# The second expert block of a fused attention and two-expert kernel: output transposed in 384-token columns, Strassen factors formed on the way in, and one list schedule for both blocks

## The chip, the cores and the metric

One core of one Trainium2 chip runs the whole program. The metric is device time in microseconds of one launch. The engines are PE (matmul, with its weight loads shown apart as PEld), DVE, ACT and POOL (elementwise work) and SP, which only issues DMAs. Each engine runs its own instructions strictly in program order and waits on the others by semaphores, so where an instruction is put on its engine decides what waits behind it.

## What is computed

```python
def _attn_ref(q, k, v):          # chunks of 64, softmax(q k / 8) v
def _moe_ref(x, w_in, w_out, g_ln):
    h = x @ w_in                 # 4608 x 512 by 512 x 1024
    solu = h * softmax(h)
    ln = (solu - mean) / sqrt(var + 1e-06) * g_ln
    return ln @ w_out            # 1024 x 512
def _moe2_ref(x, w_in, w_out):
    h = x @ w_in                 # 4608 x 512 by 512 x 2048
    g = h * (1.0 / (1.0 + np.exp(-h)))
    return g @ w_out             # 2048 x 512
```

`reference` runs the three one after the other on 4608 tokens. The four weight matrices arrive as 64-bit numbers and are turned into fp32 on the chip, in 48 pieces of 128 x 512 (512 KB each).

## The kernel before

The program has three stretches on PE. **Stage one** is attention plus the first expert block, in 36 tiles of 128 tokens: `attend`, `weigh` (softmax), `moe_in` (L499, 24 matmuls of 512 columns a tile), `norm` (L506 maximum, L510 exp, L512 product), `turn_ln` (L533 transposes) and, for every 4 tiles, four `moe_out` (L544, 24 matmuls of 512 columns each). **Way in** is the second block's first matrix product: 6 groups of 768 tokens, 8 units a group, a unit being 256 of the 2048 features. **Way out** is its second product, for 18 pairs of token tiles (256 tokens).

Every big product is done in fp32r with operands split into a high and a low part, three passes (`PASSES`: high by high, high by low, low by high); a split is one ACT copy (high) and one subtraction on DVE or POOL (low). Both products of the second block use the seven-product Strassen form (`SEVEN` = p1, p6, p2, p7, p5, p4, p3): sums of the quarter blocks of each operand are formed first, seven products are made, and their sums give the four quarters of the result.

- Weights. `convert` takes a 64-bit piece through five DVE instructions (L292, L295, L309, L314, L345) and one ACT instruction (L297). For the pieces of stage one, letters in `SUM_ON` and `LOW_ON` say whether the sum (L314) and the low part (L363) go to DVE, to POOL or through PE (E). `w2_mix` then forms the seven weight factors of two pieces on POOL (L395, four sums of 128 x 256) and splits them (L408 on ACT or L406 on POOL, and L410 on POOL), and stores both parts to HBM (`w2d`, `w2od`). The 16 pieces of the way in's matrix are done in stage one, the 16 of the way out's during the way in.
- Way in. `raw_load`, `raw_t` (L594, POOL) and `s_split` (L619 ACT, L623 DVE or POOL) make the seven operands of a group. `product` (L656) is 6 matmuls of 384 columns; a unit pair is 14 products in turn. The results are summed as they come: `c_p1` (L669), `c_u2` (L673), `c_u3` (L677), `c22` (L687), `c21` (L695), `c12` (L703), with silu on ACT. PE may write p7 only after `c_u2` has read the bank, and p3 only after `c22` has. Each unit stores four quarters of 192 KB to `gd` (L664), on SP.
- Way out. `g_load` brings the silu output back (four DMAs of 512 KB a pair), `g_sum` (L758, two on DVE and two on POOL, 128 x 1024) forms the sums, `g_split` (L769 ACT, L771 DVE or POOL) splits seven operands, and `out_product` (L778) makes 24 matmuls of 256 columns with the token block as the stationary operand:

```python
for f in range(NF):
    for i, (a, c) in enumerate(PASSES):
        nc.tensor.matmul(acc, g[:, a, f, :], wo2[o, f][:, c, :], ...
```

- Order. For stage one a planner (`Steps`, filled by `stage_one`) holds every operation with its engine, its assumed length, its needs and its due time, and `solve` list-schedules them; the start times order each engine's instructions. `NOMINAL`, `WAY_OUT` and `W2_FROM` set due times only. The way in and the way out are placed by hand, by offsets from the end of stage one (`XA`, `XB`, `FIRST_LOADS`, `FIRST_SUMS`, `FIRST_SPLITS`).

Of the kernel before, what the change touches and what calls it, by code (L numbers as in the profile page):

```python
# [43 lines left out]
class Steps:  # L44


    LATENCY = {"PE": 0.2, "DVE": 0.06, "ACT": 0.06, "POOL": 0.08, "DMA": 1.9, "SP": 0.0}
# [16 lines left out]
    def solve(self):  # L64
# [20 lines left out]
        engines = {st["engine"] for st in self.steps}  # L85
# [5 lines left out]
        while events:  # L91
# [42 lines left out]
def stage_one(T, way_out, w2_from, tiles=36, per=4, ahead=2):  # L134

    step = Steps(dict(S=1, X=1, tr=2, y=2, h=1, u=4, xs=2, e=2, pT=2, qk=3, v=2, ln=2, ys=2, st=2, cv=2, cvs=2))
    op = step.op
    dma = lambda kb, **more: ("DMA", kb * 1024 / 300e3, more)
# [5 lines left out]
    for i in range(32):  # L144
# [11 lines left out]
        due = T[w2_from] + (T[tiles - 2] - T[w2_from]) * (i - 16) / 16  # L156
        steps[-1][2].update(give=[("w", i)], due=due)
        op("convert", (i,), *steps)
        if i % 2:
            steps = [("POOL", 0.74, dict(need=[("w", i - 1), ("w", i)] if n == 0 else [])) for n in range(4)]  # L160
            for n in (512, 512, 256, 512):
                steps += [("ACT", 0.17 + n / 1200, dict(take=["cvs"])), ("POOL", 0.2 + n * 0.0021, {}), sp(n // 256 if n > 256 else 1), dma(n, free=["cvs"])]
            steps[-1][2].update(free=["cvs", "cv", "cv"], due=due + 22)
            op("w2_mix", ((i - 17) // 2, 0), *steps)
    for t in range(-ahead, tiles):
# [821 lines left out]
```

## Time and profile before

| | us |
|---|---|
| median of 3 runs (1275.37 to 1276.58) | 1276.12 |
| the profiled execution: device time | 1274.12 |
| its span, first to last instruction | 1272.3 |
| PE busy in it | 1229.5 (97%) |
| DVE, ACT, POOL busy | 794.3, 606.4, 540.5 |

The span leaves 1.8 us outside it, and the profiled execution was 2.0 us under the median. PE is the busiest engine by far; a matmul's records overlap, so the rate of a stretch is best read from the distance between the starts of equal groups.

### The profile page before, as it was taken

The numbers are of one execution on the slowest core, as the hardware profiler recorded it, in microseconds if no ns is written. First come the engines' busy times: TensorE is split into PE (matmuls) and PEld (weight loads), VectorE is DVE, ScalarE is ACT, GpSimd is POOL, SyncE is SP. The second block draws the span as 40 slices with busy tenths as digits, with TensorE's granted clock in tenths as the row PEclk, the third lists the DMA queues.
The fourth block names the chain that finished last, engine by engine and source line by source line (L and its number), as shares of the span: only waits on it lengthen the run. The fifth ranks groups of instructions, "written<-read, shape, count | busy, mean of one in ns | idle before, by whom it ended". The sixth has DMA issues, their size and how long they took to land.

```text
span 1272.3 us, 24240 instructions
## 1 busy us (share of the span) xinstructions
PE 1229.5 (97%) x9532; PEld 1126.3 (89%) x9532; DVE 794.3 (62%) x1189; ACT 606.4 (48%) x957; POOL 540.5 (42%) x525
## 2 busy tenths in 40 slices
PE   5889999999999999999999999999899999999997
PEld 3667888888888888899999999999899999999997
DVE  7899466566556553256565656553877766666661
ACT  5576555565565654344353435353434434334341
POOL 1223232332333242225553544441366766667662
PEclk9899999999999999999999999999999999999999
DMA  7343343444434326686867477769954434344320
GB/s 289 103 150 130 125 142 121 138 141 135 140 141 146 129 84 222 241 274 217 244 185 233 145 230 224 226 188 323 394 186 153 136 132 141 115 141 132 129 85 30
DMA packets 155329, 217.59 MB, mean 171 GB/s; under 512 B 11472, under 2 KB 100560, under 8 KB 155216
## 3 DMA queue, kind: packets, MB, share of 16 engines
q1 hardware_dynamic: 155216, 216.05, 51.1%
q8 instruction: 75, 1.23, 0.4%
q14 instruction: 38, 0.31, 0.1%
HBM read 130.03 MB, written 85.98 MB: 170 GB/s over the span
## 4 chain that ended last, share of the span: by engine, by line
PE 46%; DVE 2%; issue 1%; DMA 1%; POOL 1%; ACT 0%; SPq 0%; DVEq 0%
PE h L778 11%; PE hw L778 8%; PE hy L778 8%; PE h L656 7%; PE hw L656 6%; PE hy L656 6%; DMA w2od<-y1s 1%; DVE tmp L687 0%; DMA g<-gd 0%; DMA st_w<-in_w_out_dram 0%; DVE y1s L623 0%; DVE tmp L677 0%; DVE gs L771 0%; DVE tmp L673 0%; POOL y1s L410 0%
## 5 line engine op out<-in xcount | busy, mean ns | idle before, releaser
L499 PE MATMUL h<-wi,xs 128*128 128x512 f32 x864 | 216.6, 401 | 2.4 <-DVE u L512 2.4
L544 PE MATMUL yp<-lnT,wo 128*128 128x512 f32 x864 | 215.0, 399 | 0.0
L499 PEld LDWEIGHTS h<-wi,xs 128*128 128x128 f32 x864 | 161.9, 191 | 37.2 <-issue 1.9
L769 ACT ACTIVATE gs<-g 128x1024 fp32r<-128x1024 f32 x117 | 123.6, 1059 | 139.5 <-PE hw L778 61.3
L544 PEld LDWEIGHTS yp<-lnT,wo 128*128 128x128 f32 x864 | 157.6, 188 | 33.7
L656 PE MATMUL h<-y1s,w2t 128*128 128x384 f32 x864 | 162.3, 336 | 0.0
L778 PE MATMUL h<-w2o,gs 128*128 128x256 f32 x1296 | 161.5, 280 | 0.0
L771 POOL TENSOR_TENSOR gs<-g,gs 128x1024 fp32r<-128x1024 f32 x50 | 139.7, 2795 | 49.1 <-ACT gs L769 46.8
L778 PEld LDWEIGHTS h<-w2o,gs 128*128 128x128 f32 x1296 | 156.6, 189 | 0.0
L656 PEld LDWEIGHTS h<-y1s,w2t 128*128 128x128 f32 x864 | 151.5, 188 | 0.3 <-ACT tmp L669 0.2
L771 DVE TENSOR_TENSOR gs<-g,gs 128x1024 fp32r<-128x1024 f32 x67 | 115.9, 1733 | 30.0 <-ACT gs L769 28.8
L506 DVE TENSOR_REDUCE st<-h 128x1 f32<-128x1024 f32 x36 | 44.0, 1222 | 134.6 <-PE h L499 134.4
L656 PE MATMUL hw<-y1s,w2t 128*128 128x384 f32 x576 | 108.9, 337 | 5.8 <-DVE tmp L687 5.8
L778 PE MATMUL hy<-w2o,gs 128*128 128x256 f32 x864 | 111.0, 285 | 2.4 <-DVE ob L791 2.4
L778 PEld LDWEIGHTS hy<-w2o,gs 128*128 128x128 f32 x864 | 107.7, 194 | 2.6 <-ACT gs L769 2.6
L656 PE MATMUL hy<-y1s,w2t 128*128 128x384 f32 x576 | 109.2, 337 | 0.5 <-DVE tmp L673 0.4
L778 PE MATMUL hw<-w2o,gs 128*128 128x256 f32 x864 | 108.9, 282 | 0.0
L656 PEld LDWEIGHTS hw<-y1s,w2t 128*128 128x128 f32 x576 | 100.6, 188 | 8.1 <-DVE tmp L687 8.1
L778 PEld LDWEIGHTS hw<-w2o,gs 128*128 128x128 f32 x864 | 105.9, 191 | 0.0
L656 PEld LDWEIGHTS hy<-y1s,w2t 128*128 128x128 f32 x576 | 100.6, 188 | 2.9 <-DVE tmp L673 2.8
L395 POOL TENSOR_TENSOR cv<-cv 128x256 f32<-128x256 f32 x64 | 46.2, 737 | 94.7 <-DVE cv L345 85.8
L473 POOL TENSOR_TENSOR e<-e,sm 128x512 f32<-128x512 f32 x36 | 39.3, 1091 | 85.6 <-DVE st L520 28.0
(128 smaller groups left out, 1754.3 us busy)
## 6 DMA issues: line engine op xcount, KB each, us to landing
gd<-tmp SPq DMA_DIRECT2D x192, 192.0 KB
g<-gd SPq DMA_DIRECT2D x72, 512.0 KB
qk<-in_qk_dram SPq DMA_DIRECT2D x36, 512.0 KB
w2d<-cv_m SPq DMA_DIRECT2D x56, 256.0 KB
w2t<-w2d SPq DMA_DIRECT2D x56, 256.0 KB
w2od<-y1s SPq DMA_DIRECT2D x56, 256.0 KB
w2o<-w2od SPq DMA_DIRECT2D x25, 512.0 KB
st_w<-in_w_out_dram SPq DMA_DIRECT2D x24, 512.0 KB
```

Source lines behind the costliest of these rows:

```text
L395: nc.gpsimd.tensor_tensor(out=out, in0=in0, in1=in1, op=op)
L473: nc.gpsimd.tensor_tensor(out=e, in0=e, in1=sm.to_broadcast([128, HP, 2, CH]), op=ALU.mult)
L499: nc.tensor.matmul(h_t[t][:, n, :], xs[:, a, kk // 2, 128 * (kk % 2):128 * (kk % 2) + 128], wi[b][kk][:, n * 512:(n + 1) * 512], start=(kk ...
L506: nc.vector.tensor_reduce(out=mx, in_=h, axis=AX.XY, op=ALU.max, negate=True)
L544: nc.tensor.matmul(yp, wo[a][f // 4][:, f % 4, 128 * m:128 * (m + 1)], lnT[b][c][:, f, :], start=(f == 0 and i == 0), stop=(f == K1 - 1 an ...
L656: nc.tensor.matmul(acc, w[:, a, kk, :], t[:, i, c, :], start=start and kk == 0 and n == 0, stop=kk == 1 and n == 2, skip_group_check=not s ...
L769: nc.scalar.activation(out=dst[:, 0], in_=src, func=AF.Copy)
L771: (nc.gpsimd if o > (3 if v > 1 else 5) else nc.vector).tensor_tensor(out=dst[:, 1], in0=src, in1=dst[:, 0].bitcast(F32), op=ALU.subtract)
L778: nc.tensor.matmul(acc, g[:, a, f, :], wo2[o, f][:, c, :], start=start and f == 0 and i == 0, stop=f == NF - 1 and i == 2, skip_group_chec ...
```

## The change

1. The way out is transposed. The weight factor is the stationary operand and the factor of the silu output the moving one, 384 tokens wide. `out_product` is now 12 matmuls of 384 columns for two units of the inner dimension (`kp`) and both halves of 256 output columns; there are 6 groups x 7 products x 4 = 168 of them, 2016 matmuls, where there were 126 x 24 = 3024. The output leaves as (512, 4608).
2. The sums of the silu output are formed in the way in, from the quarters while they are in SBUF: per unit one on DVE and three on POOL of 128 x 384 (`g_sum`, `T_ON`). Each unit stores all seven factors, 7 x 192 KB, and the way out loads a factor (384 KB) and splits it (ACT, then always DVE); `g_sum` in the way out is gone.
3. All 32 pieces of the second block are converted and summed in stage one. The factors are stored unsplit (half the bytes); `t_load` and `w2o_load` load them and split them on the core (ACT, then DVE or POOL by `UNIT_ON`, POOL for the way out).
4. `stage_two` gives the way in and the way out to the same planner, so that one list orders all three stretches. The buffer tag `cv` has 4 buffers, `cv_s` is gone; temporaries of the way in come from `cv` too. Constants of stage one are new: due times, `LOW_ON`, `SUM_ON`.

```diff
     def w2_mix(j, right):
...
+        for n, (out_, in0, in1, op) in enumerate(((s1, x, d, ALU.add), (s3, y, z, ALU.subtract), (s2, s1, a, ALU.subtract), (s4, rest, s2, ALU.subtract))):
+            if n:
+                yield
+            nc.gpsimd.tensor_tensor(out=out_, in0=in0, in1=in1, op=op)
...
+    def split_units(pair, on):
+        (a, i), (b, j) = pair
+        runs = [a[:, i:i + 2]] if a is b else [a[:, i:i + 1], b[:, j:j + 1]]
+        for t in runs:
             yield
+            nc.scalar.activation(out=t[:, :, 0], in_=t[:, :, 1].bitcast(F32), func=AF.Copy)
+        for t in runs:
+            yield
+            low = t[:, :, 1]
+            (nc.vector if on == "D" else nc.gpsimd).tensor_tensor(out=low, in0=low.bitcast(F32), in1=t[:, :, 0].bitcast(F32), op=ALU.subtract)
...
+    def g_sum(u, n):
+        b11, b12, b21, b22 = (c_t[u, x] for x in ("p1", "u2", "u3", "c22"))
+        out, in0, in1, name = ((b11, b12, b11, "p5"), (b12, b22, b12, "p7"), (b22, b22, b11, "p6"), (b21, b21, b22, "p4"))[n]
+        (nc.vector if T_ON[n] == "D" else nc.gpsimd).tensor_tensor(out=out, in0=in0, in1=in1, op=ALU.subtract)
+        yield
+        g_store(u, name, out)
+        if n in (1, 3):
+            tmp.append(out)
...
+    def g_split(p, o, kp):
+        src = raw_g.pop((p, o, kp))
+        gs[p, o, kp] = dst = ring.pop(0)
+        nc.scalar.activation(out=dst[:, 0], in_=src, func=AF.Copy)
+        yield
+        nc.vector.tensor_tensor(out=dst[:, 1], in0=src, in1=dst[:, 0].bitcast(F32), op=ALU.subtract)
+        loads.append(src)
...
+        for i in range(2):
+            acc = bank[1000 + 2 * p + i, PLACE[SEVEN[o]]]
+            for k in range(2):
+                w = wo2[o, 2 * kp + k]
+                for n, (a, c) in enumerate(PASSES):
+                    nc.tensor.matmul(acc, w[:, a, 128 * i:128 * i + 128], g[:, c, k, :], start=start and kp == 0 and k == 0 and n == 0,
+                                     stop=kp == NF // 2 - 1 and k == 1 and n == 2, skip_group_check=not start)
...
+    stage_two(step, START, NGR, NF, TT)
...
+T_ON = 'PDPP'
...
-LOW_ON = 'EDEPDDDPEPPPEDPP'
-SUM_ON = 'DDDEDEDEEDDDDDDD'
...
+LOW_ON = 'EEEPDDDPEPEPEPDP'
+SUM_ON = 'EDEEDEDEEDDDDDDD'
```

How the list moves instructions shows at three places. In the rows, `cv` is a piece under conversion, `st_w` its raw load, `lnT` and `xs` operands of the first block, `h` and `u` the tile under the norm, `tmp` a quarter of the way in, `y1s` its operand, `ry` the raw blocks, `gs` an operand of the way out, `w2t` and `w2o` weight factors.

**DVE in stage one**, from the maximum of tile 12 (counted from 0) to that of tile 13. Before:

```order
L506 TENSOR_REDUCE st<-h 128x1
L486 TENSOR_TENSOR lnT<-tp,lnT 128x4x128
L462 TENSOR_REDUCE mx<-sx 128x8
L464 TENSOR_TENSOR e<-sx,mx 128x2x4x64
L512 SCALAR_TENSOR_TENSOR u,st<-u,h 128x1024
L513 TENSOR_SCALAR st<-st 128x1
L486 TENSOR_TENSOR xs<-sx,xs 128x512
L469 TENSOR_REDUCE sm<-e 128x8
```

and now, the first twelve rows of the same stretch:

```order
L631 TENSOR_REDUCE st<-h 128x1
L611 TENSOR_TENSOR lnT<-tp,lnT 128x4x128
L452 SCALAR_TENSOR_TENSOR cv<-st_w,cv 128x512
L637 SCALAR_TENSOR_TENSOR u,st<-u,h 128x1024
L638 TENSOR_SCALAR st<-st 128x1
L587 TENSOR_REDUCE mx<-sx 128x8
L589 TENSOR_TENSOR e<-sx,mx 128x2x4x64
L611 TENSOR_TENSOR xs<-sx,xs 128x512
L645 SCALAR_TENSOR_TENSOR st<-st 128x1
L483 SCALAR_TENSOR_TENSOR cv<-cv 128x512
L594 TENSOR_REDUCE sm<-e 128x8
L595 TENSOR_SCALAR sm<-sm 128x8
```

Before, this tile has no conversion work on DVE; now it has seven `cv` instructions, one of them between the maximum and the product (L637) that frees the PSUM tile `h` for PE.

**DVE in the way in**, about one unit pair of the fifth group. Before:

```order
L292 TENSOR_SCALAR cv<-st_w 128x512
L673 TENSOR_TENSOR tmp<-hy,tmp 128x384
L295 TENSOR_SCALAR cv<-st_w 128x512
L673 TENSOR_TENSOR tmp<-hy,tmp 128x384
L309 SCALAR_TENSOR_TENSOR cv<-st_w,cv 128x512
L314 SCALAR_TENSOR_TENSOR cv<-st_w,cv 128x512
L677 TENSOR_TENSOR tmp<-hy,tmp 128x384
L345 SCALAR_TENSOR_TENSOR cv<-cv 128x512
L677 TENSOR_TENSOR tmp<-hy,tmp 128x384
L687 TENSOR_TENSOR tmp<-hw,tmp 128x384 x2
```

and now (L819 is `c_u2`, L822 `c_u3`, L832 `c22`, L840 `c21`, L848 `c12`, L855 the `g_sum` on DVE):

```order
L822 TENSOR_TENSOR tmp<-hy,tmp 128x384 x2
L832 TENSOR_TENSOR tmp<-hw,tmp 128x384 x2
L840 TENSOR_TENSOR tmp<-h_8286,tmp 128x384
L840 TENSOR_TENSOR tmp<-h_8296,tmp 128x384
L848 TENSOR_TENSOR tmp<-hw,tmp 128x384 x2
L855 TENSOR_TENSOR tmp<-tmp 128x384 x2
L819 TENSOR_TENSOR tmp<-hy,tmp 128x384 x2
```

The conversions are gone from between the sums. The two `g_sum` of a pair (L855), each of which waits for a `g_sum` of POOL, stand on DVE ahead of `c_u2` of the next pair.

**POOL at the end of the way in and the start of the way out** (L855 `g_sum`, L711 the low part of a weight factor of the way out):

```order
L855 TENSOR_TENSOR tmp<-tmp 128x384 x13
L711 TENSOR_TENSOR w2o<-w2o 128x2x256 x6
L855 TENSOR_TENSOR tmp<-tmp 128x384 x5
L711 TENSOR_TENSOR w2o<-w2o 128x2x256 x8
L855 TENSOR_TENSOR tmp<-tmp 128x384 x5
L711 TENSOR_TENSOR w2o<-w2o 128x2x256 x7
L855 TENSOR_TENSOR tmp<-tmp 128x384 x5
```

Before, the weight factors of the way out came already split, and POOL had nothing of this there; now 21 splits stand between the last sums of the way in. PE in turn has the first four products of the way out ahead of the last two p3 of the way in.

## Rows read from the trace of the kernel before

**Rows 1.** The page, busy time of each engine (busy us, share of span, instructions).

```profile
PE 1229.5 (97%) x9532; PEld 1126.3 (89%) x9532; DVE 794.3 (62%) x1189; ACT 606.4 (48%) x957; POOL 540.5 (42%) x525
```

**Rows 2.** Windows: busy us by engine, clock, DMA share, GB/s.

```profile
64.00:96.00 32.00, 26.80 (x305) 21.28 (x304) 30.68 (x56) 23.92 (x40) 9.69 (x16) 1.00 0.44 155
...
300.00:400.00 100.00, 100.00 (x948) 82.18 (x948) 61.94 (x116) 57.40 (x92) 32.89 (x54) 1.00 0.41 140
...
600.00:700.00 100.00, 99.50 (x566) 98.11 (x565) 57.67 (x102) 42.97 (x83) 47.80 (x62) 1.00 0.72 222
...
880.00:900.00 20.00, 18.42 (x106) 18.10 (x105) 13.13 (x19) 7.99 (x15) 2.38 (x1) 1.00 1.06 385
```

**Rows 3.** Timeline of PE, start of the way in: start us, length, instruction.

```profile
539.76 2.27 PE L656 MATMUL h<-y1s,w2t 128*128 128x384 f32 x12
...
558.67 1.55 PE L656 MATMUL h<-y1s,w2t 128*128 128x384 f32 x8
```

**Rows 4.** Timeline of PE, way out: first products and the end.

```profile
901.62 3.05 PE L778 MATMUL h<-w2o,gs 128*128 128x256 f32 x24
...
918.52 4.50 PE L778 MATMUL hy<-w2o,gs 128*128 128x256 f32 x24 [2.39 <-DVE ob L791]
...
1239.77 2.96 PE L778 MATMUL h<-w2o,gs 128*128 128x256 f32 x24
...
1262.55 3.02 PE L778 MATMUL hw<-w2o,gs 128*128 128x256 f32 x24
```

**Rows 5.** Timeline of PEld, way in: the two longest waits, at a group's end.

```profile
598.71 1.35 PEld L656 LDWEIGHTS hw<-y1s,w2t 128*128 128x128 f32 x8 [2.35 <-DVE tmp L687]
...
899.43 2.03 PEld L656 LDWEIGHTS hw<-y1s,w2t 128*128 128x128 f32 x12 [1.90 <-DVE tmp L687]
```

**Rows 6.** Timeline of DVE, the maximum L506 of tiles 6, 18 and 19.

```profile
108.12 1.22 DVE L506 TENSOR_REDUCE st<-h 128x1 f32<-128x1024 f32 x1
...
273.83 1.23 DVE L506 TENSOR_REDUCE st<-h 128x1 f32<-128x1024 f32 x1 [0.93 <-PE h L499]
287.50 1.23 DVE L506 TENSOR_REDUCE st<-h 128x1 f32<-128x1024 f32 x1 [6.34 <-PE h L499]
```

**Rows 7.** Groups of DVE by form, 105 to 539 us: busy us, mean ns, idle before.

```profile
L486 DVE TENSOR_TENSOR lnT<-tp,lnT 128x512 fp32r<-128x512 f32 x64 | 43.7, 683 | 19.4 <-ACT lnT L484 18.8
...
L345 DVE SCALAR_TENSOR_TENSOR cv<-cv 128x512 f32<-128x512 f32 x16 | 11.6, 730 | 0.2
L309 DVE SCALAR_TENSOR_TENSOR cv<-st_w,cv 128x512 int32<-128x512 int32 x16 | 11.4, 721 | 2.2 <-ACT cv L297 2.2
L314 DVE SCALAR_TENSOR_TENSOR cv<-st_w,cv 128x512 f32<-128x512 uint32 x16 | 10.8, 681 | 0.0
L295 DVE TENSOR_SCALAR cv<-st_w 128x512 int32<-128x512 int32 x16 | 9.3, 581 | 0.0
L292 DVE TENSOR_SCALAR cv<-st_w 128x512 int32<-128x512 int32 x16 | 7.5, 467 | 0.0
```

**Rows 8.** Groups of POOL by form, 105 to 539 us.

```profile
L410 POOL TENSOR_TENSOR cv_m<-cv,cv_m 128x512 fp32r<-128x512 f32 x24 | 31.1, 1295 | 35.5 <-ACT cv_m L408 35.4
...
L395 POOL TENSOR_TENSOR cv<-cv 128x256 f32<-128x256 f32 x32 | 23.0, 736 | 19.6 <-DVE cv L345 11.3 <-DVE st L520 7.7
```

**Rows 9.** Groups of DVE and POOL by form, way in, 600 to 840 us.

```profile
L623 DVE TENSOR_TENSOR y1s<-ry,y1s 128x768 fp32r<-128x768 f32 x16 | 24.0, 1503 | 0.3 <-ACT y1s L619 0.3
...
L673 DVE TENSOR_TENSOR tmp<-hy,tmp 128x384 f32<-128x384 f32 x32 | 16.8, 552 | 25.4 <-issue 11.2 <-ACT y1s L619 6.4 <-PE hy L656 3.9
...
L594 POOL TENSOR_TENSOR ry<-ry 128x768 f32<-128x768 f32 x16 | 30.9, 1930 | 21.6 <-DVE y1s L623 21.4
...
L623 POOL TENSOR_TENSOR y1s<-ry,y1s 128x768 fp32r<-128x768 f32 x8 | 14.9, 1869 | 8.9 <-ACT y1s L619 8.9
```

**Rows 10.** The same split on DVE while POOL was idle, 840 to 901 us.

```profile
L623 DVE TENSOR_TENSOR y1s<-ry,y1s 128x768 fp32r<-128x768 f32 x1 | 0.9, 948 | 0.0
```

**Rows 11.** Timeline of DVE, the last instruction.

```profile
1265.60 0.42 DVE L791 TENSOR_TENSOR ob<-hw,ob 128x256 f32<-128x256 f32 x1 [2.43 <-PE hw L778]
```

More of the change, by code (lines that the diff above doesn't have):

```diff
@@ L44 @@
 class Steps:
-    LATENCY = {"PE": 0.2, "DVE": 0.06, "ACT": 0.06, "POOL": 0.08, "DMA": 1.9, "SP": 0.0}
+    LATENCY = {"PE": 0.2, "DVE": 0.06, "ACT": 0.06, "POOL": 0.08, "DMA": 1.9, "SP": 0.0, "PLAN": 0.001}
     def __init__(self, places):
@@ L143, in stage_one @@
     gap = T[-1] - T[-2]
-    for i in range(32):
+    for i in range(48):
         st, cv = ["st"] * (i >= 8), ["cv"] * (i >= 4)
@@ new lines, in chunk_attention_moe_moe, with nothing, units @@
+    PLACE = {"p1": "x", "p2": "x", "p6": "y", "p7": "y", "p5": "w", "p3": "w", "p4": "v"}
+    BUFS = {"qk": 3, "vt": 2, "e": 2, "pT": 2, "xs": 2, "wi": 2 * KD, "u": 4, "wo": 4}
+    wt, raw_y, sy, bank, tmp, c_t = {}, {}, {}, {}, [], {}
+    def nothing(*_):
+        pass
+    def units(seq):
+        out = []
+        while len(out) < 2:
+            if not seq["left"]:
+                tag, n = seq["tags"].pop(0)
+                t = sb.tile([128, n, 2, 256], F32R, tag=tag, name=seq["name"], bufs=BUFS[tag])
+                seq["left"] = [(t, i) for i in range(n)]
+            out.append(seq["left"].pop(0))
+        return out
@@ L584, in raw_load, with raw @@
+    def raw(p, i):
+        return raw_y[1][i] if p else raw_y[i]
     def raw_load(p, q):
@@ L811, in chunk_attention_moe_moe @@
+    fns = {f.__name__: f for f in (load_qk, load_v, convert, w2_mix, w2_store, nothing, attend, weigh, moe_in, norm, turn_ln, moe_out,
+                                   t_load, w2o_load, raw_places, raw_load, raw_t, s_places, s_split, spare, product, c_p1, c_u2, c_u3, c11, c22, c21, c12,
+                                   g_sum, give_back, g_places, g_load, g_split, out_product, o_p1, o_c11, o_sum)}
     plan = Plan()
@@ L834, in chunk_attention_moe_moe @@
-    x = max(step.last("w2_mix"), step.last("attend", engine="PE") - 2.0)
-    at(x, raw_places, 0)
-    for i in range(4):
-        at(x + 0.1 + 0.01 * i, raw_load, 0, i)
-    at(x + 10.0, raw_t, 0, 0)
-    at(x + 12.0, raw_t, 0, 1)
-    at(XO + 0.2, s_places, 0)
-    at(XO + 0.3, s_places, 1)
-    at(XA - 0.05, s_places, 2)
-    at(XA + PA, raw_places, 1)
-    at(XA - 0.03, spare, "st_w", 2, 2)
-    for i, (tag, bufs, n) in enumerate((("ys", 2, 1), ("ys", 2, 1), ("junk", 1, 1), ("cv_s", 2, 2), ("cv_s", 2, 2))):
-        at(XA - 0.04 + 0.001 * i if i < 4 else XA + 8.0, spare, tag, bufs, n)
```

574 lines of the change are left out of this document (275 added, 299 removed).

## Prediction

> **What bounds the kernel now.** I read the busy times of the page first. PE is busy for 97% of the span, no other engine for more than 62% [rows 1], so a gain must come from fewer or faster matmuls, or out of the 43 us in which PE stands. Next I read the timeline of PE at the seams. It shows three stretches: stage one up to 539.76, the way in from there to 901.62 [rows 3, 4], the way out to its last product, which begins at 1262.55 [rows 4], and a tail: the last sum on DVE starts at 1265.60 [rows 11], 6.7 us before the span's end.
>
> In each stretch I took the pitch between equal groups, which the overlap of matmuls can't blur. Way in: nine groups of 12 matmuls from 539.76 to 558.67 [rows 3], so 2.101 us for 12 matmuls of 384 columns, 1.05 us a product. All 336 products at that pitch are 353.0 us; the stretch lasted 361.9, so PE lost 8.9 us. Two of the waits behind that, 2.35 and 1.90 us, stand at the end of a token group, where PE waits for `c22` on DVE [rows 5]. Way out: eight products of 24 matmuls from 1239.77 to 1262.55 [rows 4], 2.848 us each; 126 of them are 358.8 us. From 901.62 to 1265.60 are 364.0 us, so 5.2 us were lost, nearly all near the start (one wait is 2.39 us, and the product behind it ran slowly [rows 4]).
>
> Stage one has two parts. Up to about 108 us DVE sets the pace: it is busy 30.68 of 32 us in the third window while PE is busy 26.80 [rows 2]. Later PE has no gap (300 to 400 us [rows 2]), and a tile takes 13.67 us from maximum to maximum [rows 6].
>
> **The change, step by step.** All sums are made against the profiled execution (span 1272.3, device time 1274.1); the median of the runs is 2.0 us above it.
>
> *Way out on PE.* 126 products of 2.848 us (358.8) go; 168 of 12 matmuls come. Their form, 384 moving columns over a 128 x 128 weight, is that of the way in, so they cost 2.101 us each: 353.0. That is **-5.8 us**; I give it 1 us either way.
>
> *Early stage one.* Ahead of the maximum of tile 6, DVE now has two sums (L314), one low part (L363) and one split (L486) less, by the order of the two programs; each is about 0.68 us [rows 7], together 2.7 us. DVE sets the pace there, but what leaves DVE there goes to PE (two sums and two low parts more), into the gaps that it has (5.2 us in the third window alone [rows 2]). I take **-2**; between -4 (latencies shrink too) and +3 (the PE work lies on the path).
>
> *Steady stage one.* 16 conversions more, at 0.467 + 0.581 + 0.721 + 0.681 + 0.730 = 3.18 us of DVE each [rows 7], are 51 us of DVE. Nothing else is so loaded: `w2_mix` loses its splits on ACT and POOL. The order puts 28 conversions into the 18 tiles from 8 to 26, where it had 10: one more a tile, 3.2 us. DVE was busy 62 of 100 us there [rows 2], 8.5 us a tile; now it is 11.7 of 13.67, 85%. The cover is the 2 us left in each tile; what is queued badly is a `cv` instruction between the maximum and the product (order above), which makes PE's single tile `h` wait 0.7 us longer. I take **+1**. The lower bound is 0, since PE has no gap to close there. For the upper bound the nearest row is the third window: DVE at 96%, PE loses 5.2 us in about three tiles [rows 2]; half a us a tile, for 18 tiles, is 9.
>
> *Way in.* PE's work is the same. DVE loses the conversions and gains one sum per unit; POOL loses `w2_mix` and gains three. A pair then holds on DVE 10 sums of 0.552 [rows 9], two of `g_sum` at about 0.55, and a quarter of the four splits of a group at 1.5 [rows 9]: 8.1 of 14.7 us. On POOL: six sums of 128 x 384 at 1.02 (between 0.736 for 256 and 1.295 for 512 columns [rows 8]), and a quarter of four `raw_t` at 1.93 and three splits at 1.87 [rows 9]: 9.5 of 14.7, 64%. Stores grow from 4 to 7 x 192 KB a unit: with the raw blocks 12.6 MB in 58.8 us, 214 GB/s. The same stretch carried 222 at a DMA share of 0.72, in rows of 512 bytes (now 1536), and 385 is reached at 880 us [rows 2]; so DMA is covered. The added wait is that of `g_sum` on DVE for POOL; behind it in DVE's queue stand `c_u2` and `c_u3` of the next pair, and PE's p7 waits for `c_u2`. The last c12 of a pair (0.552 [rows 9]) ends about 0.7 us into the next pair, silu is as much again, POOL 1.0 to 2.0, DVE 0.55: `c_u2` runs at about 4 us, and p7, the seventh product, begins at 6.3. Some 2 us are to spare, and the conversions that delayed `c22` are gone. Against that, the first pairs have few temporaries, and POOL has weight splits left. I take 7 us lost for 8.9, **-2**; between 0 lost (-9) and 1 us a pair, 24 (+15).
>
> *Start of the way out.* 21 weight splits of 1.295 us [rows 8] fall into the last three pairs on POOL: 27.2 beside 18 sums, 18.4, in 44.1 us. POOL is full there, and a late POOL sum holds DVE. PE has four products of the way out to put ahead of the last p3, and loads are halved (384 KB per 2.1 us, 187 GB/s). I take 4 us lost for 5.2, **-1**; between -5 and +6. After that a factor costs one pass on ACT and about 0.95 us on DVE [rows 10] per 2.1 us, and POOL is idle: PE is the bound.
>
> *Tail.* Two sums of 0.55 for one of 0.42 and 192 KB stores for 128: **+0.8**, 0 to +2.
>
> Sum: -5.8 - 2 + 1 - 2 - 1 + 0.8 = -9.0. Span 1263.3, device time 1265.1, with the 2.0 us to the median **1267.1**.
>
> **The port that DVE and POOL share.** In the way in, DVE's split of 128 x 768 takes 1.50 us on the mean [rows 9], 0.95 while POOL is idle [rows 10]; a sum with one input in PSUM stays at 0.552 [rows 9]. The Trainium skill, "SBUF — State Buffer", section "Who interferes with whom", says that a DVE instruction with two SBUF inputs and a POOL instruction reading SBUF take an exclusive lock, and the second waits for the whole of the first. By that rule, to which these rows agree, it speaks against this change, which puts POOL at 64% and adds `g_sum` to both engines. What it would make of the time here is the first rival.
>
> **The rivals.**
> *DVE held by POOL in the way in (slower).* Each pair has two `g_sum` on DVE that read SBUF twice, behind POOL's sums and before `c_u2`. If a `raw_t` (1.93 us [rows 9]) or a late sum comes first, `c_u2` slips past p7. At 1 us a pair, 24 us are lost in place of 8.9: the sum becomes -7.0 + 15 = +8, the time 1284; it decides from about 0.66 us a pair. For it: two engines are now coupled twice a pair, and POOL is full at the end. Against it: 2 us to spare, and a PSUM input keeps the other sums free of POOL [rows 9].
> *DVE at 85% in stage one (no change).* 9 us in place of 1: sum -1, time 1275. For it: the third window [rows 2]. Against it: there DVE was at 96%, and 2 us a tile let it catch up.
> *All waits close.* No loss in way in and way out: -9.0 - 7 - 4 = -20, time 1256. For it: one list now sees both engines, and the tiles of stage one, which it ordered, run without a gap [rows 2]. Against it: the waits at the group ends remain, since the operands of the next group are still written late.
> That the change doesn't do what it says would be a way out at another pitch than 2.10 us; the same form runs at that pitch in this trace [rows 3].
>
> **How the numbers follow.** Forecast 0.56 (its own range 1260 to 1273.5), held by POOL 0.15, stage one 0.13, all waits close 0.16. A change of 0.2% (2.6 us) is about what a measurement here can tell. Faster: nearly all of the forecast and of the last rival, a third of stage one's, together 0.71; same: 0.12; slower: most of the first rival and a third of the second, 0.17. Leaving out a tenth at each end, the range is 1254 to 1285.
>
> **What would show it.** Way-out groups of 12 matmuls 2.10 us apart and 353 to 357 us in all; 13.67 us a tile in stage one; way in 358 to 362 us with its waits at group ends, on `c22`; POOL at 60 to 70% in the way in. Wrong would be: PE waiting for `c_u2` (L819) in every pair, tiles over 14 us apart, or a way out whose loads hold PE.

## The result and the profile after

The changed kernel takes 1258.24 us (median of 4 runs, 1255.82 to 1259.76; the kernel before beside it 1276.35), a ratio of 0.985 (0.982 to 0.988). A second set of runs gave 0.985 (0.983 to 0.986). The forecast was 1267.1: right in sign, and half of the gain. The profiled execution has a span of 1254.0 us; it is 2.4 us under the median.

The stretches of PE, as in the prediction. In the changed kernel eight products of the way in stand among the last `moe_out` (8.46 us), and four of the way out ahead of the last two p3 (8.36 us); each is counted in its own stretch.

| stretch | before | forecast | after | difference |
|---|---|---|---|---|
| stage one | 539.8 | -1 | 535.3 | -4.4 |
| way in | 361.9 | -2 | 362.7 | +0.9 |
| way out | 364.0 | -6.8 | 351.7 | -12.3 |
| tail | 6.7 | +0.8 | 4.2 | -2.5 |
| sum | 1272.3 | -9.0 | 1254.0 | -18.3 |

The timeline of PE after, from which the seams are read (to be laid beside [rows 3, 4]):

```profile
518.83 2.27 PE L808 MATMUL h<-y1s,w2t 128*128 128x384 f32 x12
520.94 2.92 PE L669 MATMUL yp<-lnT,wo 128*128 128x512 f32 x12
...
543.80 1.40 PE L808 MATMUL hw<-y1s,w2t 128*128 128x384 f32 x7
...
894.96 8.51 PE L896 MATMUL h<-gs,w2o 128*128 128x384 f32 x48
903.32 1.31 PE L808 MATMUL hw<-y1s,w2t 128*128 128x384 f32 x6
905.28 1.32 PE L808 MATMUL hw<-y1s,w2t 128*128 128x384 f32 x6 [0.65 <-DVE tmp L832]
906.44 4.35 PE L896 MATMUL hy<-gs,w2o 128*128 128x384 f32 x24
```

and the last sums on DVE (against [rows 11]), 4.2 us before the end:

```profile
1249.80 1.02 DVE L921 TENSOR_TENSOR tmp<-hw,tmp 128x384 f32<-128x384 f32 x2 [5.69 <-PE hw L896]
```

The page's busy times and the windows after (columns as in [rows 1, 2]). PE is still the busiest engine; from 200 to 400 us DVE is busy 82 to 88 us of 100 where it was 59 to 62, and POOL is empty in the way out:

```profile
PE 1220.4 (97%) x8538; PEld 1114.8 (89%) x8538; DVE 813.3 (65%) x1269; ACT 629.1 (50%) x1023; POOL 457.2 (36%) x491
```

```profile
64.00:96.00 32.00, 25.72 (x247) 20.18 (x238) 28.96 (x54) 21.50 (x37) 9.14 (x15) 0.95 0.36 120
200.00:300.00 100.00, 100.00 (x895) 82.20 (x894) 87.83 (x153) 57.79 (x93) 37.95 (x59) 1.00 0.58 192
300.00:400.00 100.00, 100.00 (x949) 82.00 (x948) 81.71 (x143) 56.12 (x92) 41.31 (x61) 1.00 0.56 186
600.00:700.00 100.00, 98.36 (x563) 97.53 (x562) 55.43 (x87) 37.42 (x75) 61.60 (x51) 1.00 0.63 222
1000.00:1100.00 100.00, 100.00 (x576) 100.00 (x575) 54.20 (x66) 43.02 (x54) 0.00 (x0) 1.00 0.75 217
```

A window counts every matmul that overlaps its edges, so the pitch of the way out is read from starts, over a long stretch. After, 125 groups of 12 matmuls lie between these two starts: 2.091 us each.

```profile
982.03 2.25 PE L896 MATMUL hy<-gs,w2o 128*128 128x384 f32 x12
...
1243.35 6.41 PE L896 MATMUL hw<-gs,w2o 128*128 128x384 f32 x36
```

Before, 105 groups of 24 lie between this one and the last of [rows 4], at 1262.55: 2.855 us each.

```profile
962.75 3.02 PE L778 MATMUL hw<-w2o,gs 128*128 128x256 f32 x24
```

The maxima that mark stage one, of tiles 0, 6, 18 and 19 after (against [rows 6]):

```profile
36.59 1.17 DVE L631 TENSOR_REDUCE st<-h 128x1 f32<-128x1024 f32 x1
...
103.23 1.21 DVE L631 TENSOR_REDUCE st<-h 128x1 f32<-128x1024 f32 x1
...
269.75 1.22 DVE L631 TENSOR_REDUCE st<-h 128x1 f32<-128x1024 f32 x1 [0.24 <-PE h L624]
283.36 1.22 DVE L631 TENSOR_REDUCE st<-h 128x1 f32<-128x1024 f32 x1 [0.24 <-PE h L624]
```

and of tile 0 before:

```profile
41.91 1.23 DVE L506 TENSOR_REDUCE st<-h 128x1 f32<-128x1024 f32 x1 [2.08 <-PE h L499]
```

The weight loads of PE that wait in the way in (against [rows 5]): one of 1.14 us at each of five group starts, for `c_u2` (L819), two more of 0.4 us for it, and six for `c22` (L832), five of them in the last group. Two of them:

```profile
602.29 0.99 PEld L808 LDWEIGHTS hy<-y1s,w2t 128*128 128x128 f32 x6 [1.14 <-DVE tmp L819]
...
880.17 1.01 PEld L808 LDWEIGHTS hw<-y1s,w2t 128*128 128x128 f32 x6 [1.89 <-DVE tmp L832]
```

### The profile page after: what moved, and what is told of

Read it like the earlier page. It is cut to its first block, busy times and chain, and to the rows that moved or that the text cites. A ratio compares the mean times of both kernels' runs of the same rounds, so it can differ in the third digit from the quotient of the medians.

```text
span 1254.0 us, 22739 instructions
## 1 busy us (share of the span) xinstructions
PE 1220.4 (97%) x8538; PEld 1114.8 (89%) x8538; DVE 813.3 (65%) x1269; ACT 629.1 (50%) x1023; POOL 457.2 (36%) x491
## 4 chain that ended last, share of the span: by engine, by line
PE 95%; DVE 3%; DMA 1%; issue 0%; ACT 0%; SPq 0%; POOL 0%; DVEq 0%; POOLq 0%; ACTq 0%
PE yp L669 16%; PE h L624 15%; PE h L896 12%; PE h L808 11%; PE hw L896 8%; PE hy L896 8%; PE hy L808 8%; PE hw L808 8%; PE tp L658 2%; PE sx L570 2%; PE sx L577 1%; PE pp L602 1%; PE cs L464 1%; PE cs L465 0%; DMA w2o<-w2od 0%
## 5 line engine op out<-in xcount | busy, mean ns | idle before, releaser
L882 DVE TENSOR_TENSOR gs<-gs 128x768 fp32r<-128x768 f32 x168 | 166.8, 996 | 144.6 <-ACT gs L880 144.4
L880 ACT ACTIVATE gs<-gs 128x768 fp32r<-128x768 f32 x168 | 142.3, 847 | 176.6 <-PE h L896 61.5
L855 POOL TENSOR_TENSOR tmp<-tmp 128x384 f32<-128x384 f32 x144 | 156.8, 1108 | 109.4 <-ACT tmp L850 87.6
L896 PE MATMUL h<-gs,w2o 128*128 128x384 f32 x864 | 162.1, 336 | 0.0
L896 PEld LDWEIGHTS h<-gs,w2o 128*128 128x128 f32 x864 | 152.1, 188 | 0.0
L896 PE MATMUL hw<-gs,w2o 128*128 128x384 f32 x576 | 107.4, 336 | 0.0
L896 PE MATMUL hy<-gs,w2o 128*128 128x384 f32 x576 | 107.0, 334 | 0.0
L896 PEld LDWEIGHTS hw<-gs,w2o 128*128 128x128 f32 x576 | 100.8, 188 | 0.3 <-issue 0.3
L896 PEld LDWEIGHTS hy<-gs,w2o 128*128 128x128 f32 x576 | 100.5, 188 | 0.0
L611 DVE TENSOR_TENSOR lnT<-tp,lnT 128x512 fp32r<-128x512 f32 x72 | 49.0, 683 | 34.2 <-ACT lnT L609 34.0
```

Of the source, the lines that this page charges most:

```text
L611: nc.vector.tensor_tensor(out=lo, in0=src, in1=hi.bitcast(F32), op=ALU.subtract)
L855: (nc.vector if T_ON[n] == "D" else nc.gpsimd).tensor_tensor(out=out, in0=in0, in1=in1, op=ALU.subtract)
L880: nc.scalar.activation(out=dst[:, 0], in_=src, func=AF.Copy)
L882: nc.vector.tensor_tensor(out=dst[:, 1], in0=src, in1=dst[:, 0].bitcast(F32), op=ALU.subtract)
L896: nc.tensor.matmul(acc, w[:, a, 128 * i:128 * i + 128], g[:, c, k, :], start=start and kp == 0 and k == 0 and n == 0, stop=kp == NF // 2 - ...
```

## The experiments

Ratios are to the kernel before, measured on the same chip. Each kernel starts from the changed one unless said otherwise.

**after_again**: the changed kernel once more. 

> The changed kernel once more, as the ground for the runs beside it. Expected by its first profile: 1256 to 1260 us, tile 6's maximum at 103 us, last PE matmul to the end 4.2 us, and 13 waits of PE in the way in for L819 and L832. If the gain of 4.4 us up to tile 6 hung on the granted clock of one execution alone, the maximum of tile 6 would move by some us here.

Measured: 0.9845 (0.9828 to 0.9861). Stage one repeats to 0.1 us from tile 0 on (tile 12 comes 151.5 us after tile 0 in both, and 151.3 to 151.5 us after it in all nine profiles with this stage one). The end of the way in differs by 3 us (906.4 and 909.2): 1.2 us of it are there at tile 0 already, the rest comes with the waits for `c22` in the last pairs, where DVE waits for stores that land at other times (2.8 and 3.4 us at one `c22`). Differences of that size between two single profiles are not read.

**both_read**: where does the way in lose?

```diff
-need += {..., "p7": [("c_u2", u)], "p3": [("c22", u)]}.get(name, [])
+need += {..., "p7": [("c_u2", u), ("c_u2", u + 1 - i)], "p3": [("c22", u), ("c22", u + 1 - i)]}.get(name, [])
```

> One need more in the planner: p7 and p3 of either unit of a pair come after c_u2 and c22 of both units. Theory A: the two units of a pair share one PSUM tile (hy, hw), so that a sum of the second unit that is queued after the first unit's product waits for that product's end, and PE's next product waits for the sum; this makes the 0.8 us gap at each group start and the 0.65 us gaps at c22. Then the waits for L819 at the five group starts (1.14 us each on the weight loads) go, way in 362.7 to about 358, the time 3 to 6 us less than the changed kernel. Theory B: DVE is late at a group start because POOL holds it (g_sum 2.19 us there); then PE waits as long one product earlier, and the time stays within 1.5 us.

Measured: 0.980 (0.978 to 0.982), 5.9 us less than the changed kernel beside it. Theory A. How the wait comes about is seen in the changed kernel's timeline of all engines at 600 us: the two units of a pair lie in one PSUM tile (`hy`). The first unit's `c_u2` ran at 598.53; a `g_sum` stood between it and the second's, PE went on to p7 of the first unit, and the second `c_u2` had to wait for its end, 1.92 us, and PE's next product for `c_u2`:

```profile
598.53 0.56 DVE L819 TENSOR_TENSOR tmp<-hy,tmp 128x384 f32<-128x384 f32 x1
599.01 0.74 DVE L855 TENSOR_TENSOR tmp<-tmp 128x384 f32<-128x384 f32 x1
...
600.26 1.21 PE L808 MATMUL hy<-y1s,w2t 128*128 128x384 f32 x6
601.68 0.56 DVE L819 TENSOR_TENSOR tmp<-hy,tmp 128x384 f32<-128x384 f32 x1 [1.92 <-PE hy L808]
...
602.29 1.30 PE L808 MATMUL hy<-y1s,w2t 128*128 128x384 f32 x6 [0.82 <-DVE tmp L819]
```

With both sums ahead of both products these five waits (4.1 us) are gone, and four of 0.2 to 0.5 us are left in their place. The waits for `c22` fall from six to two, 0.35 and 0.91 us; one of 2.2 us, for `c12`, is new.

**br_pool and br_dve**: what do the shared `g_sum` cost? Both on top of both_read, with `T_ON` 'PPPP' and 'DDDD' for 'PDPP'.

> both_read with all four g_sum of a unit on POOL (T_ON PPPP): DVE has none of them and waits for no sum of POOL. POOL gets 48 sums of about 1.05 us more: in the way in 9.5 + 2.1 = 11.6 of 14.7 us a pair. Theory A (the first rival of the prediction): DVE's two g_sum a pair, which stand behind POOL's and hold the port together with them (0.71 us on the median, up to 2.2), are what the way in pays; without them it loses 2 us or more less than in both_read. Theory B: c_u2 has time to spare and the coupling costs nothing; the time stays within 1.5 us. Theory C: POOL's load decides; stores come later, temporaries come back later, and the last three pairs lose 3 to 8 us more.

> both_read with all four g_sum of a unit on DVE (T_ON DDDD): POOL keeps raw_t and the splits, DVE gets 144 sums more of 0.55 to 0.7 us, 3.4 to 4.2 us a pair: 11.5 to 12.3 of 14.7. Theory A (the coupling costs): DVE no longer waits for POOL's sums, temporaries come back sooner, the waits of the last three pairs shrink; 2 us or more below both_read. Theory B: the coupling costs nothing and DVE has room: within 1.5 us. Theory C: DVE is too full in the pairs that hold its operand splits, c_u2 and c22 come late: 3 us or more above both_read.

Measured: br_pool 0.9995 (0.998 to 1.001), 23 us above both_read; br_dve 0.9875 (0.986 to 0.989), 9 us above. Theory C both times in kind. In br_pool the loss is three times what it allowed, and most of it is not in the last pairs: PE waits 2.8 to 3.0 us for `c_u2` at three group starts and 2.1 at a fourth, where POOL also has the `raw_t` and the splits, and 4.8 us for `c22` near the end:

```profile
731.08 2.04 PEld L808 LDWEIGHTS hy<-y1s,w2t 128*128 128x128 f32 x12 [2.81 <-DVE tmp L819]
```

The coupling itself is there: DVE's `g_sum` takes 0.714 us on the median beside POOL's and 0.550 where POOL has no `g_sum` (changed kernel, then br_dve; min, median, max in ns). The stretching fits the Trainium skill, "SBUF — State Buffer", section "Who interferes with whom", by which a DVE instruction with two SBUF inputs contends with a POOL instruction that reads SBUF. The price of the coupling was not measured by itself, since both runs also move load from one engine to the other. But in both_read the weight loads wait 1.4 us for `c_u2` in the whole way in, and with the sums all on one engine the kernel was slower, not faster:

```profile
L855 DVE TENSOR_TENSOR tmp<-tmp x48: 545/714/2190, 553.3 to 936.5; 128x384 f32<-128x384 f32 x48
```

```profile
L855 DVE TENSOR_TENSOR tmp<-tmp x192: 541/550/2197, 556.3 to 927.4; 128x384 f32<-128x384 f32 x192
```

**late_start**: why did the start of the way out cost so little?

```diff
-need.append(("wo2", 4 * o + kp))
+need += [("wo2", 4 * o + kp), ("pd", NF * groups - 1, 6), ("pd", NF * groups - 2, 6)]
```

> The changed kernel with one need more: no product of the way out before the last two p3 of the way in. Theory A: the four products that the list puts there fill the wait for the last c22 and give the first factors time to arrive, and this is why the start of the way out lost 1 us where 4 were forecast; then 3 to 6 us come back at that seam and the time rises by as much. Theory B: the start is short since the loads are halved: c22 comes earlier without POOL's late splits, and the time stays within 1.5 us.

Measured: 0.993 (0.992 to 0.995), some 10 us slower than the changed kernel. Theory A, and more than it asked: PE stands 9.8 us until `c22` comes, and the 12 matmuls behind that wait take 4.0 us in place of 2.1, in a window whose granted clock is 0.50, the lower level (1.2 GHz):

```profile
904.21 4.21 PE L808 MATMUL hw<-y1s,w2t 128*128 128x384 f32 x12 [9.77 <-DVE tmp L832]
```

```profile
900.00:910.00 10.00, 5.79 (x18) 5.79 (x19) 6.10 (x10) 2.87 (x6) 3.96 (x4) 0.50 0.63 176
```

So the last `c22` is late in the changed kernel as well: the first of the two p3 could follow at 894.96 and runs at 903.32, and four products of the way out (8.36 us) fill that time.

**w2o_dve**: on top of both_read, the low parts of the way out's factors go to DVE (`split_units(pair, "D")`, and so in the list). 

> both_read with the low parts of the way out's weight factors (w2o) on DVE in place of POOL, in the list and in the code. In late_start the last p3 had to wait 9.8 us for c22; in both_read the last three pairs still hold waits of 0.9, 1.6 and 2.2 us and two slow products. Theory A: POOL is full there (21 splits of about 1.3 us and 18 sums), its late sums give temporaries back late and c22, c_p1 and c_u2 wait for them; with the splits on DVE (0.7 us each) these waits go and the time falls by 3 to 5 us against both_read (1252.7). Theory B: the temporaries come back late because of the stores on SP's queue and the DMAs behind w2o's loads; then the waits stay and the time is within 1.5 us. Theory C: the splits now stand on DVE ahead of the sums that PE waits for: 1 to 4 us slower.

Measured: 0.987 (0.985 to 0.988), 7 us above both_read. POOL has no split there any more (it is busy 16.9 of the 44 us from 862 to 906 us, 34.8 in both_read), and PE still waits 3.1 us for `c22` and 3.7 for `c_u3` in the last three pairs; DVE waits 3.75 and 4.39 us for stores that have not landed. POOL's splits alone were not the cause. The loss is more than Theory C allowed, and how much of it DVE's own splits make was not told apart.

**w2o_paced2**: on top of both_read, a weight factor is loaded only when the factor two before it has been split (in the list; no wait is added on the chip).

```diff
-op("w2o_load", (k,), sp(..., need=need + [("ol", k - 1)] * (k > 0), ...
+op("w2o_load", (k,), sp(..., need=need + [("ol", k - 1)] * (k > 0) + [("wo2", k - 2)] * (k >= 2), ...
```

> both_read with one need more in the list: the load of a weight factor of the way out comes after the split of the factor two before it, so that at most two are under way; on SP these loads then stand singly between the stores of the way in, in place of bursts of 3 to 8. Theory A: the bursts of w2o loads delay the stores gd<-tmp behind them, the temporaries come back late and c22, c_p1 and c12 of the last three pairs wait (0.9, 1.6 and 2.2 us in both_read, and two slow products): then these waits go and the time falls by 3 to 6 us against both_read (1252.7). Theory B: POOL's sums make the temporaries late, not the stores: within 1.5 us. Theory C: the factors of the way out now come too late: PE waits for w2o in the first 60 us of the way out, 2 to 6 us slower.

Measured: 1249.55 us, 0.978 (0.976 to 0.980), about 3 us below both_read, **the fastest of all**. The intervals of the two ratios overlap (0.978 to 0.982 for both_read); the times do not (1248.76 to 1250.93 against 1252.07 to 1253.35, where the kernel before took 1278.7 and 1278.8). Theory A, with a part that it did not name: pacing the loads also spreads POOL's splits. In both_read, 8 loads go out on SP in one run and 8 splits hold POOL for 10 us; the `g_sum` and stores behind them come late, DVE's `c22` waits 8.97 us for a temporary that a store still reads, and what is queued behind it on DVE holds PE at 886.50, whose next 12 matmuls are slow (from the timelines of SP, POOL, DVE and PE):

```profile
863.54 4.05 SPq L731 DMA_DIRECT2D w2o<-w2od  x8
...
869.17 10.00 POOL L711 TENSOR_TENSOR w2o<-w2o 128x512 fp32r<-128x512 f32 x8
...
878.50 1.02 DVE L832 TENSOR_TENSOR tmp<-hw,tmp 128x384 f32<-128x384 f32 x2 [8.97 <-DMA gd<-tmp]
...
886.50 3.32 PE L808 MATMUL hw<-y1s,w2t 128*128 128x384 f32 x12 [1.84 <-DVE tmp L848]
```

Paced, the longest run of splits in these pairs is two, and `c22` waits for nothing but its product:

```profile
867.93 2.80 POOL L711 TENSOR_TENSOR w2o<-w2o 128x512 fp32r<-128x512 f32 x2
...
872.30 1.02 DVE L832 TENSOR_TENSOR tmp<-hw,tmp 128x384 f32<-128x384 f32 x2 [1.06 <-PE hw L808]
```

How much of it is the loads and how much the splits was not told apart. In w2o_dve, with the bursts of loads and no split on POOL, waits of 3 us remain; but there the splits stand on DVE.

**store_2x64 and before_store_halves**: why is the tail shorter?

```diff
-out=out[m0:m0 + 128, s0:s0 + HW]
+out=out[m0:m0 + 128, s0:s0 + HW].rearrange("(a m) s -> a m s", a=2)
```

> The stores of the output are written as 2 x 64 rows in place of 128 rows, the same bytes to the same places, and nothing else. Theory A: the tail is 2.5 us shorter than before since a store whose outermost dimension is 2 goes through few DMA engines (the last store of the kernel before ran at 48 GB/s) and one of 128 rows through all (375 GB/s); then the tail rises from 4.2 to 7 to 8 us and the time by 3 to 4 us. Theory B: the tail is shorter because of longer rows (1536 for 1024 bytes) or since less is left to store; then no change within 1 us.

Measured: 0.985 (0.983 to 0.987), tail 4.2 us: nothing moved. The test was badly made: the two blocks of 64 rows follow on each other, so the pattern is the same 128 rows and can be passed on as such. In the kernel before they lie 576 rows apart. So the other way round, in the kernel before:

```diff
-nc.sync.dma_start(out=...[2 * tt:2 * tt + 2, b * CH:(b + 1) * CH, ...], in_=c)
+for h in range(2):
+    nc.sync.dma_start(out=...[2 * tt + h, b * CH:(b + 1) * CH, ...], in_=c[64 * h:64 * h + 64])
```

> The kernel before with each output store as two DMAs of 64 tokens, in place of one whose outermost dimension is 2 tokens' blocks that lie 576 rows apart; rows stay 1024 bytes. Theory A: it is that outermost dimension of 2 which keeps the last store at 48 GB/s; then the store ends about 2.5 us sooner, the tail falls from 6.7 to 4 to 4.5 us and the time by 2 to 2.7 us. Theory B: it is the shorter row or the smaller store: the tail stays at 6 us or more and the time within 1 us.

Measured: 0.998 (0.997 to 0.9995), some 2 us, with a tail of 4.9 us (last sum at 1267.26, span 1272.2) where it was 6.7. Theory A for most of it. The rate of the DMAs in 40 slices of the last 22 us before, of the last 19 after, shows what the last stores ran at: before, three stores follow on each other at some 48 GB/s for over 9 us (17 slices of 0.56); after, the last two take 1.4 us at up to 375. In before_store_halves it is up to 118 GB/s. The first row is the kernel before, the second the changed one:

```profile
GB/s 40 0 0 0 0 0 0 0 0 0 26 38 38 35 48 77 2 0 0 0 11 44 33 31 48 49 49 48 40 48 48 48 49 40 44 49 24 0 0 0
```

```profile
GB/s 17 0 0 0 0 0 0 36 369 356 42 34 0 10 16 0 0 0 65 343 10 362 49 0 0 0 0 0 0 0 0 0 0 0 294 375 159 0 0 0
```

The share of the 16 DMA engines that is busy meanwhile (last but one number; before, then after) tells why: 0.14 of 16 is two engines, 0.79 nearly 13.

```profile
1264.00:1270.00 6.00, 1.57 (x14) 1.37 (x12) 0.42 (x1) 0.00 (x0) 0.00 (x0) 0.98 0.14 47
```

```profile
1251.20:1252.60 1.40, 0.00 (x0) 0.00 (x0) 0.00 (x0) 0.00 (x0) 0.00 (x0) 1.00 0.79 281
```

In before_store_halves the share is 0.4 in the slices of a store, more than two stores of two engines each could make, so it is not only that two are under way at once. Its rows are as short as before, so Theory B can claim at most the 0.7 us between its tail and the changed kernel's.

**letters**: `SUM_ON` and `LOW_ON` as before. 

> SUM_ON and LOW_ON as in the kernel before, all else changed: two sums and two low parts go back from PE to DVE or POOL. Theory A: the letters take work off DVE, which paces the first 108 us, and give the 4.4 us; tile 6's maximum comes back to 107 to 109 us and the time rises by 4 to 5 us. Theory B: the letters give what DVE saves, 2.7 us at most (the prediction had 2), and the rest is the new list and the granted clock; the time rises by 1.5 to 2.7 us. Theory C: the whole gain is the new due times: no change within 1 us.

Measured: 0.988 (0.986 to 0.990), 3.8 us slower as a whole. But stage one ends only 0.5 us later than the mean of four profiles with the changed kernel's letters (tile 12's maximum at 189.1; 188.1 to 189.4 there), although tile 6 is 2.5 us later; the rest lies in the last pairs, where that list waits 2.2 us for `c22`. So the sums and the low part that left DVE are not what stage one gained: neither A nor B.

**stage_old and before_due**: all constants of stage one exchanged (due times, letters, `W2_FROM`, `WAY_OUT`), in the changed kernel and in the one before.

> The changed kernel with the constants of stage one as before (FIRST, the 12.9 in NOMINAL, WAY_OUT, W2_FROM, LOW_ON, SUM_ON). The letters alone moved the end of stage one by 0.5 us or less. Theory A: the due times order PE's early work so that its gaps are filled or not, and with them the clock falls: slow stretches as in the kernel before come back, tile 6's maximum at 107 us or later, the time 4 to 6 us over the changed kernel. Theory B: the gain of stage one comes from what left it (the splits of w2_mix on ACT and POOL, the cv_s tiles): tile 6's maximum stays at 103 to 105 us, the time within 1.5 us.

> The kernel before with the constants of stage one of the changed one (FIRST, the 13.87 in NOMINAL, WAY_OUT, W2_FROM, LOW_ON, SUM_ON); way in and way out stay as before. The reverse of stage_old. Theory A: what stage one gained is the order that the new due times and letters give to its first 110 us (no gap of 4.6 us at 30 us, no stretches at half clock up to 56 us), and it does not need the new second block; then stage one ends 3 to 5 us sooner, the time falls by 3 to 5 us. Theory B: the order is good only together with what left stage one (the splits of w2_mix, the cv_s tiles): within 1.5 us or slower.

Measured: stage_old 0.9965 (0.995 to 0.998), 14 us slower than the changed kernel, tile 6 at 117.6 us; before_due 1.004 (1.002 to 1.006), some 5 us slower than the kernel before, tile 6 at 117.7. Each set of constants fits only the list that it was made for: neither the due times alone nor the new list alone gives the gain. In before_due PE stands 4.95 us ahead of the attention at 39.45 us and runs slowly behind it, as the kernel before does at 35 us.

**before_fill and fill_gap**: what do PE's gaps and the clock behind them cost? In the kernel before, after a gap of 4.61 us, 12 matmuls took 4.7 us from start to start in place of 2.9 (granted clock 0.50 from 36 to 40 us); the changed kernel has no such gap there, and its first 24 matmuls of `moe_in` run at full clock (timeline of PE, before, then after):

```profile
35.08 1.13 PE L445 MATMUL sx<-pT,vt 64*64 64x64 f32 x32 [4.61 <-ACT wi L354]
35.96 1.10 PE L452 MATMUL sx<-qk 64*64 64x64 f32 x32
36.99 4.88 PE L499 MATMUL h<-wi,xs 128*128 128x512 f32 x12
```

```profile
30.10 6.08 PE L624 MATMUL h<-wi,xs 128*128 128x512 f32 x24
...
74.99 7.34 PE L624 MATMUL h<-wi,xs 128*128 128x512 f32 x24 [2.70 <-DVE u L637]
```

before_fill adds matmuls to the attention and one conversion of the kernel before:

```diff
+for _ in range({2: 24, 1: 3}.get(t, 0)):
+    nc.tensor.matmul(sx[:, 0, 256:384], ident, ident, start=True, stop=True)
```

> The kernel before with 37 extra matmuls of 128 columns on PE whose results are overwritten: 10 ahead of the second E sum (in the gap of 1.98 us at 14.3 us), 24 ahead of the second and 3 ahead of the third attention product (in the gap of 4.61 us at 30.5 us and the one of 0.69 us at 42.3). Theory A: in the kernel before PE's gaps were followed by stretches at half clock (17 to 20.5, 35 to 41.5, 47 to 51 us, 6.7 us of work lost against 1.7 in the changed kernel), and most of the 4.4 us that stage one gained is this; with the gaps filled the clock stays up at least from 16 to 42 us, tile 6's maximum comes from 108.1 to 103 to 106 us and the time falls by 2 to 5 us. Theory B: DVE sets the pace of the first 108 us, PE's slow stretches lie beside it and cost nothing: tile 6's maximum stays within 1 us, the time within 1.5.

Measured: 1.003 (1.0015 to 1.004), tile 6 at 114.55, 6.4 us later. A miss: the 24 extra matmuls needed the tile `sx`, which DVE gave free only at 35.09, so they did not fill the gap but followed it, at half clock (8.39 us). The ten in the first gap did keep the clock at 1.00 from 16 to 24 us, and PE's next chain began at 28.05 where it had begun at 28.08: that slow stretch had cost nothing. fill_gap uses a free tile in the changed kernel:

```diff
+if t == 4:
+    acc = ps.tile([128, CW], F32, tag="y", name="fill", bufs=2)
+    for _ in range(14):
+        nc.tensor.matmul(acc[:, 0:128], ident, ident, start=True, stop=True)
```

> The changed kernel with 14 extra matmuls of 128 columns, whose result nobody reads, ahead of tile 4's moe_in, in the gap of 2.7 us at 72.3 us in which PE waits for the product L637. After that gap the 24 matmuls of tile 4 took 7.34 us in place of 5.75, at a granted clock of 0.79 from 72 to 80 us. Theory A: the idle gap lowers the clock and the slow matmuls lie on the path: the 24 matmuls take 5.8 us, the maximum of tile 4, counted from that of tile 0, comes 1 to 1.6 us sooner (45.8 us in the changed kernel), that of tile 12 (151.5) 0.5 to 1.6. Theory B: DVE sets the pace there: the 24 matmuls are faster, but tile 12 does not move by more than 0.3 us.

Measured: 0.987 (0.985 to 0.989); the whole time says nothing here, since its last pairs waited longer. In stage one, the matmuls of tile 4 take 5.76 us, tile 4's maximum comes 1.3 us sooner after tile 0's (44.5 for 45.8 us), and the clock falls one gap later: tile 5 takes 7.30 us. Tile 12 gains 0.4 us (it comes 151.05 us after tile 0, and 151.25 to 151.54 in the nine profiles without the filling). Half of each theory:

```profile
72.86 3.29 PE L621 MATMUL fill<-ident 128*128 128x128 f32 x28
75.91 5.76 PE L628 MATMUL h<-wi,xs 128*128 128x512 f32 x24
...
86.01 7.30 PE L628 MATMUL h<-wi,xs 128*128 128x512 f32 x24 [2.23 <-DVE u L641]
```

## Why the prediction was right in sign and short by half

Four terms (stage one taken as one) came out better than forecast, by 2.7 to 3.4 us each, and one worse, by 2.9; together they are the 9.3 us that were missed.

**Way out on PE (-5.8).** Right in kind, too small in size: measured -8.5. The step that failed is the pitch of both forms, each read from eight or nine groups. The 2.101 us come from the first groups of the way in, at 540 us; over a long stretch the form goes at 2.091, so 168 products are 351.2 us and not 353.0. The 2.848 us come from the last groups of the way out; over 105 groups they are 2.855, so the 126 products that went were 359.8 us and not 358.8.

**Start of the way out (4 us lost for 5.2).** With these pitches 4.2 us were lost before and 351.7 - 351.2 = 0.5 us now, -3.7 in place of -1. That POOL is nearly full in the last pairs (38.4 of 44 us from 862 to 906 us) and `c22` late was right (the wait is 9.8 us in late_start), though w2o_dve does not bear out that the one makes the other. The step that failed is that I let PE pay for it: I named the four products that the list puts there and did not subtract their 8.36 us from the wait.

**Tail (+0.8).** Measured -2.5. The step counted the sums and the bytes of the last store (192 for 128 KB) and never asked at which rate it goes. [rows 11] shows 6.7 us from the start of a sum of 0.42 us to the end: the 6 us that are left are the store, its start and its landing included. The Trainium skill, "DMA: Bandwidth & Descriptors", section "Why a DMA increments its semaphore by 16 and not by 1", says that a transfer uses the largest number of engines up to 16 that divides the slowest dimension of both sides; for 2 blocks of 64 tokens that is 2. The trace agrees: 0.14 of 16 engines busy, at 48 GB/s, an eighth of the 385 of [rows 2]. With that section read against the store, the term was to be had in advance.

**Early stage one (-2).** Measured: tile 6 comes 4.9 us sooner (108.12 in [rows 6], 103.23 now), stage one ends 4.4 sooner. The step that failed is that DVE's instructions were counted and nothing else: letters gave three of the four back to DVE, and stage one lost 0.5 us. All of the gain lies ahead of tile 0 (41.91 before, 36.59 now; from there to tile 6 it is 66.2 us before and 66.6 now), where PE before has the gap of 4.6 us at 30 us and the slow matmuls behind it. That this order of PE's work is the gain fits the traces; that it can't be had from due times and letters alone is shown (before_due). An early tile 0 alone is not it either: in letters and in stage_old it comes at 33.9, and tile 6 at 106.2 and 117.6. The gain is known to some 2 us only, since before_store_halves, whose stage one is that of the kernel before, has tile 6 at 110.16:

```profile
110.16 1.23 DVE L506 TENSOR_REDUCE st<-h 128x1 f32<-128x1024 f32 x1 [1.27 <-PE h L499]
```

What the clock's part is stays open. At one place 1.6 us of slow matmuls were worth 0.4 us at tile 12 (fill_gap), at another nothing (before_fill). The kernel before and before_store_halves, which share one stage one, point both ways too: tile 0 comes at 41.9 in both, although the granted clock up to 42 us is 0.88 in the first and 0.92 in the second; tile 6 comes 2 us later in before_store_halves, where the clock from 42 to 110 us is 0.95 in place of 0.97. So the cause of this term stays open.

**Steady stage one (+1).** Right: 13.61 us a tile from tile 18 to 19 (13.67 before), PE without a gap, with DVE busy 82 to 88% of the time (85% forecast); from tile 6 to tile 35 it is 397.0 us for 397.2. The rival that DVE at 85% costs 9 us fell. Its 9 us do not follow from the row they name: 5.2 us in about three tiles are 1.7 us a tile, not half a us, and 31 for 18 tiles.

**Way in (-2).** Measured +0.9: 9.7 us lost at the prediction's pitch, for 7. The step that failed is "some 2 us are to spare": in a steady pair they were, where PE hardly waits, but at a group start the list put the second unit's `c_u2` behind a `g_sum` and so behind a product in the same PSUM tile: five times 0.82 us on PE. both_read shows it by taking it away. At group starts the list has L819 and L855 in turn, so it was visible before any run; I had put the waits at the group ends and on `c22` instead.

**The rivals.** DVE held by POOL: the stretched `g_sum` are there, but PE waits for `c_u2` at the group starts and hardly in the pairs between, and the five waits of 0.82 us went without moving a sum (both_read). The point from which POOL decides is close all the same, one sum more per unit brought 23 us (br_pool). All waits close, 1256: the time is near by luck, the way is not; waits in the way in stayed, and the gain that made up for them came from the tail, the pitch and stage one, which that rival did not have.

## What to carry to other kernels

Price every seam and the tail by its own rows, above all the last store by its rate, since nothing hides it; a store whose outermost dimension is 2 ran at an eighth of the rate of one with 128. When a list fills a wait with other work, subtract that work from the wait before charging it. Where two results share one PSUM tile, read both before writing either again, and pace loads whose follow-up work holds an engine that others wait for: these two needs in the planner took some 8 us more off (0.978 of the kernel before for 0.985). Constants fitted by hand to one list do not carry over to another that looks alike: exchanging them cost 5 to 14 us in either direction (before_due, stage_old), more than most of the terms of this prediction. And read a pitch from starts that lie a hundred groups apart, not from nine groups or from a window's count.

## What the runs showed of the hardware

- The granted clock was 0.50 behind a wait of PE of 9.8 us, and the next 12 matmuls took 4.0 us in place of 2.1 (late_start); behind waits of 2.2 and 2.7 us in stage one, 24 matmuls took 7.3 us in place of 5.76 (granted clock 0.79 from 72 to 80 us), but not behind each such wait (5.77 us behind one of 2.16): filling one gap moved the fall to the next (fill_gap).
- Over 125 groups of the way out, one fp32r matmul of 384 columns takes 174.2 ns (2.091 us for 12), and one of 256 columns 119.0 ns before (2.855 us for 24).
- A store whose outermost dimension is 2 kept 0.14 of the 16 DMA engines busy, at 48 GB/s; one of 128 rows 0.79, at up to 375 GB/s.
